# Attention reads and a SoLU feed-forward on one core: w_out split by halves of columns, two tiles turned by TensorE, and a new written-out order

## The chip, the cores and the metric

The kernel runs on one core of a Trainium2 chip. A core has a matrix engine (TensorE, here PE, with PEld for its weight loads), three engines that work on rows of 128 partitions (VectorE or DVE, ScalarE or ACT, GpSimd or POOL), a queue that issues DMA transfers (SyncE, SP), an on-chip memory and eight banks of accumulators that PE writes. Each engine takes its instructions in program order; semaphores tie the engines together. The metric is the device time of one execution in microseconds, lower is better.

## What is computed

```python
def _attn_ref(x, state):                       # x: 8 x 8 x 512 x 64, state: 8 x 8 x 32 x 64
    scores = scale * np.matmul(x, state.transpose(0, 1, 3, 2))
    a = softmax(scores)                        # over the 32 states
    xread = np.matmul(a, state)
    scores2 = scale * np.matmul(state, x.transpose(0, 1, 3, 2))
    a2 = softmax(scores2)                      # over the 512 tokens
    sread = np.matmul(a2, x)
    return np.concatenate([xread, sread], axis=2)

def _moe_ref(x, w_in, w_out, g_ln):            # 4608 rows, 512 -> 1024 -> 512
    h = x @ w_in
    solu = h * softmax(h)
    ln = (solu - mean(solu)) / np.sqrt(var(solu) + 1e-06) * g_ln
    return ln @ w_out
```

The rows of the second function are the reads of the first, heads side by side: 512 token reads and 32 state reads for each of 8 batches. All values are float32, the weights float64.

## The kernel before

The rows are cut into 34 tiles of 128: four tiles of token reads for each batch (tile t belongs to batch t // 4) and two tiles (32, 33) with the state reads of all batches. The token reads are never formed: since xread @ w_in = a @ (state @ w_in), the kernel multiplies the state of each batch with w_in once (V) and takes a from there to h. The work of each tile or batch is a generator, a "step", and the text ORDER names them in the order in which the program is to issue them; `X*n` advances step X n times. No scheduler moves anything after that: what stands earlier in ORDER stands earlier in the queue of its engine. PLACES gives each buffer its slot, and OPT says for each kind of work which engine does which instance (a for ACT, d for DVE, p for POOL). The steps are:

- l, cl, c: a load of half a weight chunk (`raw`, l0 to l7 from w_in, l8 to l15 from w_out), its low words on ACT (L220), and its conversion from float64 on DVE (L231, L234) with an addition on DVE or POOL (L237) into `wf`.
- Ls, LT, Ln, Lg: loads of state, of x in two layouts, and of g (`gT`).
- V{b}{n}: state of batch b times half n of w_in, in two groups of matmuls on PE (L187), each evicted from the accumulators into `swf` (batches 0 and 1) or `vt`. For batches 2 to 7 Y writes that to DRAM, Z reads it back and P splits it into a high and a low part (`swh`, `swl`).
- S{b}: scores on PE (two groups, also L187). A{b}, or Ah{b}{part} for batch 0: the softmax over states on DVE, ACT and POOL, ending in the transposed `aT` (DVE) and, but for batch 0, its parts `ath` and `atl`. E{b}: the softmax over tokens, whose result goes through DRAM; R{b} multiplies it with x (`srps`).
- H{t}: the first product of a tile into an accumulator of two banks (L477), in plain float32 for tiles 0 to 3 and in three products of high and low parts for the others.
- C{t}: from h to the normalised u (maximum on DVE L484, exponential on ACT L487, product on DVE L490, subtraction of the mean L495 or L497, squares on ACT L502, four small steps on POOL L504 to L507).
- D{t}: `bounce`. DVE transposes u in blocks of 32 (`ub`, L514), one DMA writes it to DRAM (`ut`), one reads it back in another layout (`back`).
- T{t}: splits `back` into `uh` and `ul`, in two halves. O{t}: the second product, 24 matmuls of 512 columns into one bank (L545), an eviction with the row scale (`osb`, L552 or L554), and the transfer to the output. Tile 33 does it in two halves of 256 columns.
- wo{f}: the split of chunk f of w_out, scaled by g: `wohi` on ACT (L267), `wolo` on DVE (L271). wp and wi do the same for w_in, which only the last two tiles need.
- K: one small matmul of `ident` with itself (`warm`, L569) whose result nobody reads. It stands where PE would otherwise be idle.

Accumulators: four banks serve h and the V groups of batches 0 and 1, as two buffers of two banks; four serve everything else on PE.

Of the kernel before, what the change touches and what calls it, by code (L numbers as in the profile page):

```python
# [8 lines left out]
F32 = mybir.dt.float32  # L9
# [19 lines left out]
OPT = dict(ph=2, k4=45, direct=[0, 1], hn=[0], vh=[0, 1], ah=[0], add='dpdpdpdpppppppdp', whi='aadd', wlo='dppp',  # L29
           ev='daaaaaaaadaaadaaaaaaaaaaaaaaaaaa', swh='aaaaaaaaadaaaaaa', swl='pppppppppppdddpd', sub='dppddppd',  # L30
           subh='dpdddpdddpdddpdd', mulh='dddddpdddpdddpdd', mul='ppppdpdd', ath='aaaaaddd', alo='dpppppdp',
           up='aaaaaaaaddaaadaaaaaaaaddaadadadadd',
           uh='aaaaaaaadaaaddaaaaaaaaaaadaadaaadaaadaddaaaadaaddaaddadddadaaadadaaa',
           ul='ppddppppdpdppppppddppdppppddpppdpdpppdppppppppdppppdpppdddddppdddddd',
           oe='aaaaaaaaaaaaaadadaaaadadaaaaadaada', hs='aaaaaaaa', jit=[], ed=[0, 1], ec='aaaaaaaaaaaaaaaa')
# [7 lines left out]
c9 c15 c9 c13 E0 cl11 c11 cl8 c8 Lg*2 c13 H0 P10 Ah01 LT20 C0*2 S1 A1*3 Ln00 A1 C0 E1*3 V41 K LT21 cl14 cl9 P11 H1*2
C1 Y31 c9 V41*2 wo4 A1*4 V41 Lg C1*2 V51 K Y21 H3*2 C0*2 D0 C3 V51 C1 D1*2 A1 V51*2 D0 V61 C3 H2*2 C3 R0*2 P10 cl15
Y51 C2 V61 R0 V61 D1 A1 S2 C3 D3 c15 C2*2 wo0 wo2 wo3 wo2 A1 D0 H4*3 c14 H4*3 H5*2 wo1 wo0 wo1 wo3 D3 V61 H5 wo5 H5*3
Z20 c14 T1*2 E1 T1 wo4 O1*2 wo6 O1 wo7 O1*3 wo5 Y50 wo6 C2 T0 T1 C3 D3 O1*3 wo7 T0*2 D2 O0 T0 wp2 O0*2 E2*2 O0 O1 E1
A2 D2 O1*2 E1 O0*5 A2*2 O0*2 C1 T3 Y40 C1 O1 T3*2 LT30 E1*2 C4*2 D2 E2 C0 E2*2 LT31 O0*2 E1 C2 Ln11 T3 E1 O1 A2 E1
Ln10 O3*2 C4*2 O3*2 C5 T2*3 D4*2 C5 E1 C5 A2 O3 R0 O3*5 E2 O0 D4 T2 O3*2 H6*2 A2*2 C2 C3 C5 O2*3 E2 C4 D5*2 wp3 C5 Z21
H6*2 A2 H6*2 wp2 O3*2 P20*2 H7*2 O2*3 C6*3 O2 C6 O2*5 A2 O2 T4 D5 T4 Y41 C5 T4 H7*3 D6*2 H7 C7 O2 S3 R1*3 O4 T4 O4*4
R1 O4*2 wp3 A2 A3*2 P21 C7*2 O4*2 T5 H8*2 Ln21 A2 O4*3 A3 T5 D6 C6 H9*2 C7 D7*2 E2 P21 T5 E2 Z30 H9*2 O5*4 H9*2 D7 E2  # L50
C4 O4 E3 LT40 E3*4 A3*2 LT41 T5 C9*2 T6*2 O5*2 C7 C9*3 D9 O5 H8 O5*2 C7 T6*2 O5 H8*2 A3*2 H8 O5*3 O6*2 O4 O6 P30 O6 D9
O6*2 E3*3 T7 H10*5 T7*3 A3 C8 O6*3 C8*2 O7 C8*2 D8 C6 Z31 P31 O7 Ln20 P31 O6 D9 O6*2 H10 O6 E3 O6 O7*4 A3 C10 O7 D8
# [24 lines left out]
T33*2 O30*3 T30 O30*2 O29 C30 O30 C33 T29 O30 T33 O33*5 T32 O33*3 O29*3 T32 O33*3 T32 O33 C33 O33*9 O32*6 C29*2 O32*4
T32 O32*2 O33 O29*2 C32*2 O32*2 O33*6
# [25 lines left out]
def attention_then_solu_ffn(ctx, tc, xT, xn, stB, w_in, w_out, g, out):  # L104
# [11 lines left out]
    SLOTS = dict(s2=2, m1=1, z1=1, r=1, sc=2, rr=3)  # L116
# [535 lines left out]
```

## Time and profile before

| | |
|---|---|
| device time, median of 3 runs | 352.25 us (350.67 to 353.64) |
| the profiled execution | 350.98 us |
| its span, first to last instruction | 349.2 us |
| busy share: PE, DVE, ACT, POOL | 97%, 79%, 63%, 52% |
| DMA, mean over the span | 270 GB/s |

Busy time is a union over instructions. On PE the end of a matmul is modelled, so prices of matmuls are better taken from start to start. A float32 matmul with float32 operands leaves two records in the profile, one of the split kind (fp32r operands) leaves one. In rows of the timeline equal instructions that follow each other are merged, with their count behind x, and a wait stands in brackets with what ended it.

### The profile page before, as it was taken

What the parts mean: (1) busy time and instruction counts of PE and PEld (TensorE: products, weight loads), DVE (VectorE), ACT (ScalarE), POOL (GpSimd) and SP (SyncE); (2) the same over time, 40 slices, a digit from 0 to 9 for tenths busy, and PEclk for the clock granted to TensorE, in tenths of its full rate; (3) what the DMA queues carried; (4) which work ended last, traced back from release to release, by engine and by line L of the source; (5) the groups of instructions that cost most, each with busy time, mean ns of one, the idle gap of its engine ahead of it and who ended that gap; (6) DMA issues with size and microseconds to landing.
All of it is one profiled execution on the core that took longest, in us unless ns stands there. A gap on an engine that the chain in (4) does not pass through costs nothing.

```text
span 349.2 us, 6119 instructions
## 1 busy us (share of the span) xinstructions
PE 339.0 (97%) x2220; PEld 255.5 (73%) x2220; DVE 274.9 (79%) x386; ACT 220.6 (63%) x356; POOL 182.7 (52%) x241
## 2 busy tenths in 40 slices
PE   5999999999999999999999999999999999999995
PEld 4343335888788867888878778887888888888894
DVE  3889999997888778998779897888787896555720
ACT  3579999889658567578565676555863463544250
POOL 0063594378756764678579463444455518412220
PEclk9899999999999999999999999999999999999999
DMA  7996998899998899999997976897897345344432
GB/s 240 416 402 268 342 322 269 307 294 343 294 363 272 339 363 332 312 329 310 340 327 263 323 247 215 288 306 288 270 297 255 113 150 212 115 167 172 150 107 75
DMA packets 47854, 94.25 MB, mean 270 GB/s; under 512 B 4432, under 2 KB 26192, under 8 KB 47824
## 3 DMA queue, kind: packets, MB, share of 16 engines
q1 hardware_dynamic: 47824, 93.87, 77.8%
q8 instruction: 17, 0.28, 0.3%
q14 instruction: 13, 0.11, 0.1%
HBM read 54.53 MB, written 37.22 MB: 263 GB/s over the span
## 4 chain that ended last, share of the span: by engine, by line
PE 43%; DVE 20%; DMA 15%; ACT 11%; issue 4%; POOL 4%; SPq 1%; DVEq 0%; ACTq 0%; POOLq 0%
PE o L545 28%; PE h L477 13%; DMA back<-ut 7%; DMA out_dram<-osb 3%; DVE u L490 2%; DMA raw<-w_in_dram 2%; DVE sm L484 2%; ACT u L495 2%; DVE wf L234 2%; DVE ub L514 2%; ACT e L487 2%; ACT uh L142 2%; DMA ut<-ub 2%; POOL ul L147 1%; DVE aT L408 1%
## 5 line engine op out<-in xcount | busy, mean ns | idle before, releaser
L147 POOL TENSOR_TENSOR ul<-back,uh 128x512 fp32r<-128x512 f32 x43 | 58.8, 1373 | 66.4 <-ACT uh L142 40.1
L545 PE MATMUL o<-wohi,uh 128*128 128x512 f32 (+1 forms) x280 | 74.8, 385 | 0.6 <-ACT uh L142 0.4
L545 PE MATMUL o<-wolo,uh 128*128 128x512 f32 (+1 forms) x280 | 75.3, 383 | 0.0
L545 PE MATMUL o<-wohi,ul 128*128 128x512 f32 (+1 forms) x280 | 73.6, 383 | 0.0
L545 PEld LDWEIGHTS o<-wohi,uh 128*128 128x128 f32 x280 | 51.5, 188 | 12.1 <-ACT uh L142 1.3
L545 PEld LDWEIGHTS o<-wolo,uh 128*128 128x128 f32 x280 | 51.8, 188 | 10.4
L545 PEld LDWEIGHTS o<-wohi,ul 128*128 128x128 f32 x280 | 51.7, 188 | 10.3
L490 DVE SCALAR_TENSOR_TENSOR u<-h,e 128x1024 f32<-128x1024 f32 x34 | 41.4, 1217 | 22.1 <-ACT e L487 21.2
L487 ACT ACTIVATE e<-h,sm 128x1024 f32<-128x1024 f32 x34 | 37.9, 1113 | 29.0 <-DVE sm L484 28.7
L514 DVE STREAM_TRANSPOSE ub<-u 128x1024 f32<-128x1024 f32 x34 | 42.1, 1237 | 8.3 <-ACT u L495 7.9
L484 DVE TENSOR_REDUCE sm<-h 128x1 f32<-128x1024 f32 x34 | 41.0, 1207 | 8.5 <-PE h L477 4.6
L502 ACT ACTIVATE e<-u 128x1024 f32<-128x1024 f32 x34 | 35.9, 1056 | 9.5 <-DVE u L497 9.2
L142 ACT ACTIVATE uh<-back 128x512 fp32r<-128x512 f32 x48 | 29.0, 623 | 17.2 <-DMA back<-ut 17.2
L495 ACT ACTIVATE u<-u,sm 128x1024 f32<-128x1024 f32 x24 | 27.6, 1149 | 16.4 <-DVE u L490 16.3
L552 ACT ACTIVATE osb<-o,sm 128x512 f32<-128x512 f32 (+1 forms) x29 | 19.2, 663 | 25.4 <-PE o L545 12.1
L477 PE MATMUL h<-swh,ath 128*128 128x512 f32 x112 | 35.1, 395 | 0.0
L477 PE MATMUL h<-swl,ath 128*128 128x512 f32 x112 | 34.5, 389 | 0.0
L477 PE MATMUL h<-swh,atl 128*128 128x512 f32 x112 | 34.5, 389 | 0.0
L237 POOL TENSOR_TENSOR wf<-wf,r 128x512 uint32<-128x512 uint32 x11 | 14.0, 1290 | 27.7 <-DVE wf L234 23.9
L147 POOL TENSOR_TENSOR swl<-swf,swh 128x1024 fp32r<-128x1024 f32 x10 | 24.3, 2432 | 8.0 <-ACT swh L142 5.2
L477 PEld LDWEIGHTS h<-swh,ath 128*128 128x128 f32 x112 | 20.6, 188 | 5.3 <-ACT e L487 0.8
L477 PEld LDWEIGHTS h<-swl,ath 128*128 128x128 f32 x112 | 21.0, 188 | 4.5
(86 smaller groups left out, 496.8 us busy)
## 6 DMA issues: line engine op xcount, KB each, us to landing
ut<-ub SPq DMA_DIRECT2D x34, 512.0 KB, 3.1
back<-ut SPq DMA_DIRECT2D x34, 512.0 KB, 4.9
out_dram<-osb SPq DMA_DIRECT2D x33, 256.0 KB, 4.7
xT<-xT_dram SPq DMA_DIRECT2D x16, 512.0 KB, 8.0
xn<-xn_dram SPq DMA_DIRECT2D x16, 512.0 KB, 7.7
kept<-vt SPq DMA_DIRECT2D x12, 512.0 KB, 6.3
swf<-kept SPq DMA_DIRECT2D x12, 512.0 KB, 6.3
raw<-w_in_dram SPq DMA_DIRECT2D x8, 512.0 KB, 8.4
```

The source lines that it names most:

```text
L142: nc.scalar.activation(out, src, AF.Copy)
L147: engine(k).tensor_tensor(out=out, in0=a, in1=hi.bitcast(F32), op=ALU.subtract)
L237: engine(of("add", n)).tensor_tensor(out=w, in0=w, in1=rounding[n], op=ALU.add)
L477: nc.tensor.matmul(ph[t][:, cols], left[l][:, p, tok], weights[:, cols], start=(p, l, r) == (0, 0, 0), stop=(p, l, r) == (parts - 1, *kind ...
L484: nc.vector.tensor_reduce(nm, ph[t], AX.X, ALU.max, negate=True)
L487: nc.scalar.activation(e, ph[t], AF.Exp, bias=nm, accum_out=z)
L490: nc.vector.scalar_tensor_tensor(out=u, in0=ph[t], scalar=-1.0, in1=e, op0=ALU.mult, op1=ALU.mult, accum_out=su)
L495: nc.scalar.activation(u, u, AF.Identity, bias=su, scale=-float(DF))
L502: nc.scalar.activation(e, u, AF.Square, scale=float(DF) ** -0.5, accum_out=ss)
L514: nc.vector.transpose(ub, us[t][0])
L545: nc.tensor.matmul(po, ut[t][l][:, f, :], w[NP + f // 2][:, f % 2, cols], start=(hf, l, w is wohi, q) == (0, 0, True, 0), stop=(hf, l, q) ...
L552: nc.scalar.activation(o[:, cols], po, AF.Copy, scale=us[t][1])
```

## The change

w_out is loaded and split by halves of its columns, not by chunks of its rows: l8 to l11 now bring the left 256 columns of all eight chunks, l12 to l15 the right 256. wo{m} has three steps: a multiplication by g in place on DVE or POOL, the high part on ACT, the low part on DVE or POOL. Tiles 0 to 3 form their second product in halves, each with its own bank, output buffer and transfer, as tile 33 did. For tiles 0 and 1, D is not `bounce` but `turn_on_pe`: C writes u with its columns permuted (`pu`), PE multiplies its eight chunks with `ident`, and ACT copies the result to `back`. The state is loaded by quarters, not halves. Who does what (OPT), the buffers' slots (PLACES) and the whole order are new.

```diff
-OPT = dict(ph=2, k4=45, direct=[0, 1], hn=[0], vh=[0, 1], ah=[0], add='dpdpdpdpppppppdp', whi='aadd', wlo='dppp',
-           ev='daaaaaaaadaaadaaaaaaaaaaaaaaaaaa', swh='aaaaaaaaadaaaaaa', swl='pppppppppppdddpd', sub='dppddppd',
+OPT = dict(ph=2, k4=45, direct=[0, 1], hn=[0], vh=[0, 1], ah=[0], add='dpppdpddpddddddp', whi='dapd', wlo='ppdd',
+           ev='aaaaaaaaaaaaaaaaaaaaaaaaaaaaaaaa', swh='aaaaaaaappappaad', swl='pppdppdpdpppdppd', sub='ddpppppp',
...
+           oe='aaaaaaaaaaaaaaaaaaaaaaaaaaadaddaaa', jit=[], ed=[0, 1], ec='aaaaaaaaaaaaaaaa', oh=[0, 1, 2, 3, 33],
+           pt=[0, 1], tb='aaaaaaaaaaaaaaaaaaaaaaaaaaaaaaaaaaaaaaaaaaaaaaaaaaaaaaaaaaaaaaaaaaaa', wg='pdddpppd',
+           woh='aaaaaaaa', wol='pddpdddp')
...
-K*5 l0 c0 l2 c2 K*6 c0 c2 cl0 c0 cl2 Ls0 c2 V10 K*3 l6 c6*2 l4 cl6 V20 K V00 K c4*2 cl4 c6 l7 cl7 c4 V00 V20*2 c7*2 l1
+K*2 l2 c2*2 l0 K c0*2 K*5 cl0 cl2 K*2 l6 K c0 K c6*2 Ls0 K l4 K*2 cl6 cl4 K c6 LT00 c2 V00 K*2 c4 K*2 c4 K c4 V10 LT01
...
         else:
-            src = w_out.bitcast(U32).rearrange("(p c f) h -> c f p h", p=4, f=NS)[n - 2 * NP]
-            nc.sync.dma_start(raw[n].rearrange("p h k -> p (h k)"), src)
+            half, i = divmod(n - 2 * NP, NP)
+            src = w_out.bitcast(U32).rearrange("(p c f) h -> c f p h", p=4, f=NS)
+            for c in range(2):
+                nc.sync.dma_start(raw[n].rearrange("p (c h) k -> p c (h k)", c=2)[:, c],
+                                  src[2 * i + c, :, :, half * DM:(half + 1) * DM])
...
+    def split_w_out(m):
+        half, i = divmod(m, NP)
...
+        w = wf[NP + m // 2][:, m % 2].rearrange("p (c h) -> p c h", c=2)
+        engine(of("wg", m)).tensor_tensor(out=w, in0=w, in1=gT[:, 2 * i:2 * i + 2, None].broadcast_to(w.shape), op=ALU.mult)
+        yield
+        hi, lo = (x[NP + i][:, :, half * DM // 2:(half + 1) * DM // 2] for x in (wohi, wolo))
+        copy(of("woh", m), hi, w)
+        yield
+        minus(of("wol", m), lo, w, hi)
+        yield
...
         k = of("up", t)
+        v, into, src = u, u, u
+        if t in OPT["pt"]:
+            v = block([DF], F32, f"pu{t}")
+            into = v.rearrange("x (c f p) -> x p c f", p=4, f=NS)
+            src = u.rearrange("x (p c f) -> x p c f", p=4, f=NS)
         if k == "a":
-            nc.scalar.activation(u, u, AF.Identity, bias=su, scale=-float(DF))
+            nc.scalar.activation(into, src, AF.Identity, bias=su, scale=-float(DF))
...
+    def turn_on_pe(t):
+
+        cols = us[t][0].rearrange("x (c m) -> x c m", c=NFC)
+        for hf in range(2):
+            ps = bank([NFC // 2, P], f"tp{t}_{hf}")
+            for c in range(NFC // 2):
+                nc.tensor.matmul(ps[:, c, :], cols[:, hf * NFC // 2 + c], ident, start=True, stop=True)
+            yield
+            if hf == 0:
+                back[t] = block([NFC, P], F32, f"back{t}")
+            copy(of("tb", 2 * t + hf), back[t][:, hf * NFC // 2:(hf + 1) * NFC // 2], ps)
+            yield
...
-        width = DM // 2 if t == NTILES - 1 else DM
+        width = DM // 2 if t in OPT["oh"] else DM
...
-        step(f"D{t}", bounce, t)
+        step(f"D{t}", turn_on_pe if t in OPT["pt"] else bounce, t)
```

What this moves on the engines, at the two places that matter below. First, PE ahead of the first second product. Before, the last V group and the scores of batch 2 (`sps2`) came there, and then the twelve matmuls each of h4 and h5, of which the first four are shown:

```order
L187 MATMUL swps6_1_1_596<-wf2_151,st2_228 32x512 x2
L187 MATMUL swps6_1_1_596<-wf3_127,st2_228 32x512 x2
L187 MATMUL sps2_0_662<-xT2_0_484,st0_112 32x512 x4
L187 MATMUL sps2_1_663<-xT2_1_522,st0_112 32x512 x4
L477 MATMUL h4_692<-swh1_0_480,ath1_660 128x512 x2
L477 MATMUL h4_692<-swl1_0_643,ath1_660 128x512 x2
L477 MATMUL h4_692<-swh1_0_480,atl1_688 128x512 x2
L477 MATMUL h4_692<-swh1_1_439,ath1_660 128x512 x2
```

Now PE turns tiles 0 and 1 (`tp`) in the middle of h2 and goes on to the second product of tile 1:

```order
L483 MATMUL h2_677<-swf0_0_134,aT0_1_513 128x512 x2
L539 MATMUL tp0_0_693<-ident_74,pu0_609 128x128 x4
L539 MATMUL tp0_1_700<-ident_74,pu0_609 128x128 x4
L539 MATMUL tp1_1_711<-ident_74,pu1_517 128x128 x4
L573 MATMUL o1_0_716<-wohi4_429,uh1_623 128x256 x2
L483 MATMUL h2_677<-swf0_1_135,aT0_1_513 128x512 x2
L573 MATMUL o1_0_716<-wohi5_686,uh1_623 128x256 x2
```

The scores of batch 2, h4 and h5 have moved behind the first halves of the second products of tiles 1 and 0.

Second, DVE from the last exponential of tile 1 on. Before:

```order
L490 SCALAR_TENSOR_TENSOR u1_558,sm1_535<-h1_530,e1_556 128x1024
L514 STREAM_TRANSPOSE ub0_576<-u0_508 128x1024
L484 TENSOR_REDUCE sm3_578<-h3_569 128x1
L514 STREAM_TRANSPOSE ub1_585<-u1_558 128x1024
L408 STREAM_TRANSPOSE aT1_0_589<-a1_0_500 128x1024
L490 SCALAR_TENSOR_TENSOR u3_608,sm3_578<-h3_569,e3_601 128x1024
L484 TENSOR_REDUCE sm2_649<-h2_603 128x1
```

Now, at the place where the softmax of batch 1 (`a1`, `aT1`, `atl1`) ends:

```order
L151 TENSOR_TENSOR ul1_705<-back1_586,uh1_623 128x512
L151 TENSOR_TENSOR wolo5_687<-wf4_317,wohi5_686 128x2x256
L151 TENSOR_TENSOR wolo6_634<-wf5_467,wohi6_633 128x2x256
L411 TENSOR_TENSOR a1_0_276<-a1_0_276,z1_1_0_556 128x1024
L496 SCALAR_TENSOR_TENSOR u3_764,sm3_636<-h3_547,e3_691 128x1024
L414 STREAM_TRANSPOSE aT1_0_782<-a1_0_276 128x1024
L490 TENSOR_REDUCE sm2_788<-h2_677 128x1
L525 STREAM_TRANSPOSE ub3_790<-u3_764 128x1024
L366 TENSOR_REDUCE sc1_264<-se1_265 128x1
L151 TENSOR_TENSOR atl1_816<-aT1_0_782,ath1_786 128x1024
```

The transposes `ub0` and `ub1` are gone, and the end of batch 1's softmax, with its last product now on DVE, has moved behind a part of the split of w_out.

More of the change, by code (lines that the diff above doesn't have):

```diff
@@ L43 @@
[L43 to L52, printed above, removed]
@@ L257, in split_w_in @@
         yield
-    def split_w_out(f):
-        n, q = NP + f // 2, f % 2
-        if q == 0:
-            wohi[n] = block([2, DM], F32R, f"wohi{n}")
-            wolo[n] = block([2, DM], F32R, f"wolo{n}")
-        w, by, hi, lo = wf[n][:, q], gT[:, f:f + 1], wohi[n][:, q], wolo[n][:, q]
-        if of("hs", f) == "a":
-            nc.scalar.activation(hi, w, AF.Copy, scale=by)
-        else:
-            nc.vector.tensor_scalar_mul(hi, w, by)
+    def split_w_out(m):
+        half, i = divmod(m, NP)
+        if half == 0:
+            wohi[NP + i] = block([2, DM], F32R, f"wohi{NP + i}")
+            wolo[NP + i] = block([2, DM], F32R, f"wolo{NP + i}")
+        w = wf[NP + m // 2][:, m % 2].rearrange("p (c h) -> p c h", c=2)
+        engine(of("wg", m)).tensor_tensor(out=w, in0=w, in1=gT[:, 2 * i:2 * i + 2, None].broadcast_to(w.shape), op=ALU.mult)
         yield
-        nc.vector.scalar_tensor_tensor(out=lo, in0=w, scalar=by, in1=hi.bitcast(F32), op0=ALU.mult, op1=ALU.subtract)
+        hi, lo = (x[NP + i][:, :, half * DM // 2:(half + 1) * DM // 2] for x in (wohi, wolo))
+        copy(of("woh", m), hi, w)
+        yield
+        minus(of("wol", m), lo, w, hi)
         yield
@@ L493, in chain @@
         k = of("up", t)
+        v, into, src = u, u, u
[3 more added lines that the diff above has]
+            src = u.rearrange("x (p c f) -> x p c f", p=4, f=NS)
         if k == "a":
-            nc.scalar.activation(u, u, AF.Identity, bias=su, scale=-float(DF))
+            nc.scalar.activation(into, src, AF.Identity, bias=su, scale=-float(DF))
         else:
-            engine(k).tensor_scalar(out=u, in0=u, scalar1=-float(DF), scalar2=su, op0=ALU.mult, op1=ALU.add)
-        us[t] = (u, r)
+            engine(k).tensor_scalar(out=into, in0=src, scalar1=-float(DF), scalar2=su, op0=ALU.mult, op1=ALU.add)
+        us[t] = (v, r)
         yield
-        nc.scalar.activation(e, u, AF.Square, scale=float(DF) ** -0.5, accum_out=ss)
+        nc.scalar.activation(e, v, AF.Square, scale=float(DF) ** -0.5, accum_out=ss)
         yield
@@ L520, in bounce @@
         yield
+    def turn_on_pe(t):
[9 more added lines that the diff above has]
+            yield
     def t_steps(t):
         for hf in range(2):
-            src = back[t].rearrange("p (q c s) -> p c q s", q=4, c=NFC)[:, 4 * hf:4 * hf + 4]
-            part = lambda x: x.rearrange("p c (q s) -> p c q s", q=4)[:, 4 * hf:4 * hf + 4]
+            if t in OPT["pt"]:
+                src = back[t][:, 4 * hf:4 * hf + 4]
+                part = lambda x: x[:, 4 * hf:4 * hf + 4]
+            else:
+                src = back[t].rearrange("p (q c s) -> p c q s", q=4, c=NFC)[:, 4 * hf:4 * hf + 4]
+                part = lambda x: x.rearrange("p c (q s) -> p c q s", q=4)[:, 4 * hf:4 * hf + 4]
             if hf == 0:
@@ L557, in o_steps @@
                 row = (t // NT) * ROWS + (t % NT) * P
-                nc.sync.dma_start(out[row:row + P, cols], o[:, cols])
+                nc.sync.dma_start(out[row:row + P, cols], o)
             else:
@@ L561, in o_steps @@
                 rows = out.rearrange("(b r) d -> r b d", r=ROWS)[S:, b:b + P // NS, cols]
-                nc.sync.dma_start(rows, o[:, cols])
+                nc.sync.dma_start(rows, o)
             yield
@@ L583, in attention_then_solu_ffn @@
         step(f"wo{f}", split_w_out, f)
-    for k in (0, 2):
+    for k in range(B // 2):
         step(f"Ls{k}", load_st, k)
```

112 lines of the change are left out of this document (61 added, 51 removed).

## The prediction

> **What bounds the kernel now.** I read the busy time by stage first, then the waits of TensorE (PE), then its timeline, because PE is the engine with the largest share. Stages, in us from the start of the span (columns: length, then busy time and count of PE, PE's weight loads, DVE, ACT, POOL, then granted clock, DMA share, GB/s):
>
> ```profile
> 8.23:18.37 10.14, 9.34 (x66) 3.16 (x66) 9.07 (x16) 5.26 (x8) 1.62 (x2) 0.83 1.02 412
> 18.37:57.39 39.02, 38.19 (x380) 14.96 (x381) 37.41 (x62) 35.80 (x63) 24.58 (x19) 1.00 0.88 327
> 57.39:345.00 287.61, 287.04 (x1756) 233.21 (x1752) 225.68 (x305) 176.37 (x282) 155.81 (x216) 1.00 0.77 261
> ```
>
> From 57.39 us on PE lacks 0.6 us of being busy all the time; from 18.37 to 57.39 PE, DVE and ACT are all close to full. The list of PE's own waits says the same; these are its longest before and its longest after that point:
>
> ```profile
> PE swph L187 <- DVE wf L237: 2.5, 1, 2.5
> ...
> PE o L545 <- ACT uh L142: 0.4, 1, 0.4
> ```
>
> So after the first loads the end is set by what stands in PE's queue, which runs in program order: a matmul that is added there costs its full price, and a transfer or a DVE instruction that is taken away gives nothing unless PE waited for it. What can still be gained lies ahead of 57 us, in the start and in the filler matmuls (`warm`, step K), which take PE's time like any other. PE's timeline in that part (start, length, line, names, shape, count; a float32 matmul leaves two records, so 10 records of `warm` are five K):
>
> ```profile
> 1.34 4.35 PE L569 MATMUL warm<-ident 128*128 128x128 f32 x22 [1.34 <-POOL ident masks.py:199]
> 8.23 2.52 PE L187 MATMUL swph<-wf,st 64*32 64x512 f32 x8 [2.54 <-DVE wf L237]
> 10.68 1.36 PE L569 MATMUL warm<-ident 128*128 128x128 f32 x6
> ...
> 18.37 1.19 PE L187 MATMUL sps<-xT,st 64*32 64x512 f32 x16 [0.80 <-ACT vt L142]
> ...
> 21.44 1.06 PE L187 MATMUL swps<-wf,st 64*32 64x512 f32 x8
> 22.43 0.94 PE L569 MATMUL warm<-ident 128*128 128x128 f32 x6
> ...
> 25.17 1.38 PE L569 MATMUL warm<-ident 128*128 128x128 f32 x10
> 26.48 1.09 PE L187 MATMUL swps<-wf,st 64*32 64x512 f32 x16
> ...
> 29.22 0.49 PE L569 MATMUL warm<-ident 128*128 128x128 f32 x2
> 29.64 1.09 PE L187 MATMUL swps<-wf,st 64*32 64x512 f32 x16
> 30.66 0.49 PE L569 MATMUL warm<-ident 128*128 128x128 f32 x2
> 30.98 1.88 PE L477 MATMUL h<-swf,aT 128*128 128x512 f32 x4
> 32.80 1.92 PE L187 MATMUL swps<-wf,st 64*32 64x512 f32 x24
> 34.65 0.71 PE L569 MATMUL warm<-ident 128*128 128x128 f32 x4
> ...
> 40.40 3.60 PE L477 MATMUL h<-swf,aT 128*128 128x512 f32 x8
> 43.93 1.09 PE L187 MATMUL swps<-wf,st 64*32 64x512 f32 x16
> ...
> 53.45 1.10 PE L432 MATMUL srps<-xn,e 128*32 128x64 f32 x64
> ...
> 57.39 0.73 PE L477 MATMUL h<-swh,ath 128*128 128x512 f32 x2
> ...
> 62.96 1.07 PE L545 MATMUL o<-wohi,uh 128*128 128x512 f32 x4
> ```
>
> Prices, from start to next start: a run of K costs 0.42 us for one (29.22 to 29.64) and 1.31 for five (25.17 to 26.48), so 0.42 + 0.22 for each further one, 1.09 for four. A V or S group of 8 records costs 0.99 alone (21.44 to 22.43); two in a row 1.02 (29.64 to 30.66), three 1.85 (32.80 to 34.65), and the six from 26.48 to 29.22 2.74, because neighbours overlap. An h tile of batch 0 costs 3.53 (40.40 to 43.93), half of one 1.82 (30.98 to 32.80), R0 1.1. The first second-product matmul (o) starts at 62.96.
>
> The second products at the end of the kernel, where both widths stand side by side:
>
> ```profile
> 329.19 1.07 PE L545 MATMUL o<-wohi,uh 128*128 128x512 f32 x4
> 330.10 1.07 PE L545 MATMUL o<-wolo,uh 128*128 128x512 f32 x4
> ...
> 335.67 0.64 PE L545 MATMUL o<-wolo,uh 128*128 128x256 f32 x4
> ...
> 337.58 0.64 PE L545 MATMUL o<-wohi,ul 128*128 128x256 f32 x4
> ...
> 344.48 0.64 PE L545 MATMUL o<-wohi,ul 128*128 128x256 f32 x4
> ```
>
> A 512-wide matmul costs 0.91 / 4 = 0.227 us, a 256-wide one (337.58 - 335.67) / 16 = 0.119: two halves cost 0.239. The last matmul ends at 344.48 + 0.64 = 345.1; the span ends 4.1 later, at 349.2.
>
> **The change, part by part.**
>
> *Halves.* Tiles 0 to 3 issue 48 narrow matmuls for 24 wide ones: 48 x 0.119 - 24 x 0.227 = 0.27 us each, 1.1 us for four, all of it in PE's full stretch. Their evictions and output transfers are split too; those lie beside PE.
>
> *Turning on PE.* 16 matmuls of 128x128 float32 against `ident`, the form of K: four after half of h3, twelve ahead of the first o. By the K price 1.09 + (0.42 + 11 x 0.2225) = 4.0 us on PE. What it takes away (two DVE transposes of `ub`, four DRAM transfers for tiles 0 and 1) was not what PE waited for: PE spent 57.39 to 62.96 on h4 and h5.
>
> *Fillers.* K stands 41 times instead of 34. Five of the added seven lie ahead of the first V, where PE is idle anyway; behind the first V there are 25 instead of 23, about 0.4 us.
>
> *Loads at the start.* The state comes by quarters and x of batch 0 moves up behind four weight loads. A load of 512 KB lands every 1.33 us in these two waits of ACT, for the fourth and the fifth load:
>
> ```profile
> 9.56 0.68 ACT L220 ACTIVATE r<-raw 128x512 uint32<-128x512 uint32 x1 [2.95 <-DMA raw<-w_in_dram]
> 10.89 0.68 ACT L220 ACTIVATE r<-raw 128x512 uint32<-128x512 uint32 x1 [0.65 <-DMA raw<-w_in_dram]
> ```
>
> S0 now needs 6.5 loads (three weights, half a state load, a weight, two of x): 10.89 + 1.5 x 1.3 = 12.8 us, where S0 started at 18.37. PE's own queue reaches S0 at 12.4 if nothing waits: first V at 8.5 (the same loads and conversions as for 8.23), 0.99, five K 1.31, 0.99, two K 0.64. I take 12.8.
>
> *The clock.* The first V above cost 2.45 us (8.23 to 10.68) for the 0.99 of 21.44, and the clock of that stage was 0.83: PE had stood still for 2.54 us and the clock was cut. With 16 K, at 0.21 to 0.11 us a record, PE now runs to about 6.5 and stands still for 2.0 us. If the clock is cut again, the first V costs 2.45 and the five K some 1.7, and S0 comes at 14.3. The Trainium skill, TensorE: Matmul & The Clock Gate, Part 1, says that the clock falls back after an idle window of about 3.4 us; by that rule neither gap would cut it and S0 stays at 12.8. The trace of before disagrees in its 2.54 us, so the shorter gap stays open. I take the clock as held, three to one.
>
> *From S0 to the first o on PE*, counted in the new order: 22 V and S groups in runs of 2, 1, 3, 2, 1, 1, 1, 6, 3, 2 (13.5 us), 18 K in nine runs (5.8), then h1, h0, both halves of h3 and one of h2 (12.5), four runs of three V groups (7.4), R0 (1.1) and the turns (4.0): 44.2 us. First o at 12.8 + 44.2 = 57.0.
>
> *From there to the end.* Behind its first o, before needed 345.1 - 62.96 = 282.2 us. The new order still has S2 (1.0), h4 and h5 (62.96 - 57.39 = 5.6), the other half of h2 (1.8) and the 1.1 of the halves: 291.7. Last matmul 57.0 + 291.7 = 348.7, which is 3.6 us later than 345.1; with the clock cut 5.1 later. If the one later wait of 0.4 us goes, 3.2. Weighted: +3.8.
>
> *Does DVE deliver in time?* It was full from its first softmax transpose to the first ul; the two rows between show what its kinds cost, 0.63 for a 512-wide transpose (38.00 to 38.63), up to 1.2 where 1024 columns are read:
>
> ```profile
> 19.50 1.44 DVE L388 STREAM_TRANSPOSE a<-sps 128x256 f32<-128x256 f32 x4 [1.11 <-PE sps L187]
> ...
> 38.00 0.70 DVE L408 STREAM_TRANSPOSE aT<-a 128x512 f32<-128x512 f32 x1
> 38.63 1.18 DVE L484 TENSOR_REDUCE sm<-h 128x1 f32<-128x1024 f32 x1
> ...
> 62.50 0.68 DVE L147 TENSOR_TENSOR ul<-back,uh 128x512 fp32r<-128x512 f32 x1
> ```
>
> Priced by kind, that stretch comes to 41.8 us and took 43.0, 3% more. In the new order `atl1`, which h4 needs, is the 81st DVE instruction from the first softmax transpose: about 36 of 512 columns at 0.6, 16 of 1024 at 1.06 to 1.21, 12 conversions at 0.45, eight transposes of 0.36 to 0.63, nine small ones: 51 us, with the 3% 52.4. From 13.8 it comes at 66.2. PE asks for it at 57.0 + 1.8 + 46 x 0.119 + 1.0 + four matmuls of h4 (0.9) = 66.2. No slack: 0 to 1.5 us of wait, which stands in the range. Before, `aT1` stood ahead of the w_out split on DVE; now it stands behind part of it.
>
> *The scattered write of pu.* ACT now writes u of tiles 0 and 1 with neighbours 16 bytes apart. The nearest rows are the same pass with adjacent elements and the one ACT copy that reads scattered elements:
>
> ```profile
> L495 ACT ACTIVATE u<-u,sm 128x1024 f32<-128x1024 f32 x24 | 27.6, 1149 | 16.4 <-DVE u L490 16.3
> ...
> L142 ACT ACTIVATE xrh<-sreadT x1: 2095/2095/2095, 279.9 to 279.9; 128x1024 fp32r<-128x1024 f32 x1
> ```
>
> So 1.15 to 2.1 us each, and I take 2.1, the scattered one: 1.9 us more on ACT for both. The Trainium skill, SBUF — State Buffer, section on the DMA port swizzle, says that SBUF lines are 16 bytes and that each access to a new line pays; by it every element pays, the sum would be the 2.1, and the row of xrh agrees in kind. PE reaches the first turn 12.1 us behind the start of h1 (12.8 + 19.2 + 12.1 = 44.1), while u1, 27 us of DVE instructions behind 13.8, is due at about 41, so this costs PE nothing; it can delay e0 and through it DVE by up to 1 us.
>
> *The rest* (shares between DVE, ACT and POOL, w_out's three-step split, smaller out tiles, casts of uh on POOL) lies beside a full PE; its cover is PE's queue, and if that runs dry it shows as the second rival.
>
> **The rivals.**
> First, the sum stands: +2.6 (no later wait, clock held, S0 at 12.4) to +5.5 us.
> Second, supply fails behind 65 us. The way of a tile through DRAM and back, from the DMA issues (size, median us to landing):
>
> ```profile
> ut<-ub SPq DMA_DIRECT2D x34, 512.0 KB, 3.1
> back<-ut SPq DMA_DIRECT2D x34, 512.0 KB, 4.9
> ```
>
> `ub3` now comes on DVE two places behind `aT1`, at about 65, so its data are back near 74; PE has h4, h5 and o of tiles 0 and 1 until about 76. With 2 us of slack there, and casts on POOL whose duration no row shows, one or two late tiles would add 2 to 5 us: +6 to +10. For it: DVE was 37.4 of 39 us busy; against it: before, with such slacks, only 0.6 us was lost behind 57 us.
> Third, not slower: the 16 turns take one pass, not two, each 0.11 us, 2 us less, and with a held clock and the 0.4 us wait gone the sum is +1.2 us, within 1%. It decides if tp leaves one record for each matmul. Against it: K has the same shape and leaves two (68 records, 34 K). The Trainium skill, TensorE: Matmul & The Clock Gate, Terms, gives float32 a transpose mode four times faster; the code issues a plain matmul, and no run here shows that mode.
> Fourth, faster: the earlier first o (57.0 against 62.96) would count in full, -6 us. It does not, since h4 and h5 only change places with it.
>
> **How the numbers follow.** The profiled execution took 350.98 us around its span of 349.2; the median of the three runs is 352.25, 1.3 more. 352.25 + 3.8 = 356.0. About 1% (3.5 us) is what a measurement of this kernel can tell from no change. Chances: first case 0.62, of which two fifths stay within 3.5 us; second 0.22; third 0.12; faster by over 1% 0.04. So same 0.25 + 0.12 = 0.37, slower 0.37 + 0.22 = 0.59, faster 0.04. Range: from +0.9 (third case, a little below) to +9 (most of the second): 353.1 to 361.5; the first case alone 354.8 to 357.8.
>
> **What would show it.** Right: the first o at 56 to 59 us, sps of batch 0 at 12.4 to 14.3, 32 tp records of 0.11 us, PE busy from there to the end, last matmul 348 to 350. Wrong: PE waiting on uh or ath behind 65 us (second), tp in 16 records (third), or PE's end ahead of 345.

## The result, and the profile after

| | before | after |
|---|---|---|
| device time, median of 4 runs each, taken together | 352.94 us (350.67 to 354.25) | 356.56 us (355.62 to 359.24) |
| after / before, 95% interval | | 1.0115 (1.0072 to 1.0158) |
| the profiled execution | 350.98 us | 355.69 us |
| its span | 349.2 us | 353.9 us |
| last matmul ends | 345.1 us | 350.4 us |

The change makes the kernel 1.15% slower. By the trace PE ends 5.3 us later, and the stretch behind its last matmul is 0.6 us shorter (3.5 for 4.1 us), which leaves 4.7 in the span.

The stages of after, cut at the first V, at the scores of batch 0 and at the first second product (length, then busy time of PE, its weight loads, DVE, ACT, POOL, then granted clock, DMA share, GB/s):

```profile
9.97:15.52 5.55, 5.55 (x31) 3.04 (x31) 2.58 (x5) 1.18 (x2) 0.00 (x0) 0.69 1.03 416
15.52:60.06 44.54, 44.15 (x434) 18.93 (x433) 42.51 (x74) 40.04 (x70) 16.16 (x14) 1.00 0.83 298
60.06:350.40 290.34, 290.34 (x1871) 239.38 (x1869) 222.42 (x291) 168.91 (x273) 192.54 (x252) 1.00 0.73 254
```

From its first second product to its last matmul PE of after is never idle. The list of all of PE's waits is three rows long, and the last of them ends at 26 us:

```profile
PE swph L191 <- DMA st<-stB_dram: 2.1, 1, 2.1
PE warm L596 <- POOL ident masks.py:199: 1.3, 1, 1.3
PE swps L191 <- DVE a L394: 0.4, 1, 0.4
```

So the chain that ended last, in which PE held less than half before, is now almost all PE (share by engine, from the pages of before and of after):

```profile
PE 43%; DVE 20%; DMA 15%; ACT 11%; issue 4%; POOL 4%; SPq 1%; DVEq 0%; ACTq 0%; POOLq 0%
```

```profile
PE 95%; DMA 2%; ACT 1%; SPq 0%; issue 0%; DVE 0%
```

PE's timeline of after, with the rows on which the prediction's times are to be read:

```profile
1.34 6.49 PE L596 MATMUL warm<-ident 128*128 128x128 f32 x32 [1.34 <-POOL ident masks.py:199]
9.97 1.62 PE L191 MATMUL swph<-wf,st 64*32 64x512 f32 x8 [2.14 <-DMA st<-stB_dram]
11.52 2.44 PE L596 MATMUL warm<-ident 128*128 128x128 f32 x10
13.88 1.06 PE L191 MATMUL swph<-wf,st 64*32 64x512 f32 x8
14.88 0.71 PE L596 MATMUL warm<-ident 128*128 128x128 f32 x4
15.52 1.09 PE L191 MATMUL sps<-xT,st 64*32 64x512 f32 x16
...
35.22 3.70 PE L483 MATMUL h<-swf,aT 128*128 128x512 f32 x8
...
48.01 1.05 PE L539 MATMUL tp<-ident,pu 128*128 128x128 f32 x8
48.99 1.92 PE L191 MATMUL swps<-wf,st 64*32 64x512 f32 x24
...
57.46 2.84 PE L539 MATMUL tp<-ident,pu 128*128 128x128 f32 x24
60.06 0.48 PE L573 MATMUL o<-wohi,uh 128*128 128x256 f32 x2
```

The turns take 48.99 - 48.01 = 0.98 and 60.06 - 57.46 = 2.60 us, together 3.58. The first V starts 1.74 us later than before (9.97 for 8.23), and five fillers right behind it take 13.88 - 11.52 = 2.36 us, where five took 1.31 at the full clock. The ledger of the 5.3 us comes from adding up PE's rows by kind, each from its start to the next start:

| | us |
|---|---|
| first V later | +1.7 |
| turns | +3.6 |
| second products (narrow +23.5, wide -22.3) | +1.2 |
| fillers behind the first V, 25 for 23 | +1.4 |
| V groups +0.6, scores -0.8, first products -0.6 | -0.8 |
| waits behind the first V, 0.4 for 2.2 | -1.8 |
| sum | +5.3 |

### The profile page after: what moved, and what is told of

The parts are those of the page before. It is cut to its first block, busy times and chain, and to the rows that moved or that the text cites. A ratio compares the mean times of both kernels' runs of the same rounds, so it can differ in the third digit from the quotient of the medians.

```text
span 353.9 us, 6463 instructions
## 1 busy us (share of the span) xinstructions
PE 346.5 (98%) x2362; PEld 267.7 (76%) x2362; DVE 272.5 (77%) x375; ACT 213.8 (60%) x348; POOL 211.2 (60%) x274
## 4 chain that ended last, share of the span: by engine, by line
PE 95%; DMA 2%; ACT 1%; SPq 0%; issue 0%; DVE 0%
PE o L573 53%; PE h L483 29%; PE swps L191 4%; PE srps L438 2%; DMA st<-stB_dram 2%; PE sps L191 2%; PE warm L596 2%; PE swph L191 2%; PE tp L539 1%; SPq L212 0%; ACT vt L146 0%; DVE a L394 0%; ACT se L372 0%; ACT r L227 0%; ACT a L403 0%
## 5 line engine op out<-in xcount | busy, mean ns | idle before, releaser
L151 POOL TENSOR_TENSOR ul<-back,uh 128x512 fp32r<-128x512 f32 x49 | 67.5, 1381 | 46.5 <-ACT uh L146 25.4
L573 PE MATMUL o<-wohi,ul 128*128 128x512 f32 (+1 forms) x312 | 76.1, 362 | 0.0
L573 PEld LDWEIGHTS o<-wohi,uh 128*128 128x128 f32 x312 | 54.8, 189 | 9.8 <-issue 0.5
L573 PEld LDWEIGHTS o<-wohi,ul 128*128 128x128 f32 x312 | 54.9, 189 | 9.5
L573 PEld LDWEIGHTS o<-wolo,uh 128*128 128x128 f32 x312 | 54.3, 189 | 9.0
L496 DVE SCALAR_TENSOR_TENSOR u<-h,e 128x1024 f32<-128x1024 f32 x34 | 41.4, 1217 | 16.8 <-ACT e L493 13.9
L525 DVE STREAM_TRANSPOSE ub<-u 128x1024 f32<-128x1024 f32 x32 | 39.6, 1238 | 7.4 <-ACT u L506 6.5
L579 ACT ACTIVATE osb<-o,sm 128x512 f32<-128x512 f32 (+1 forms) x36 | 22.4, 623 | 31.9 <-PE o L573 20.7
L146 ACT ACTIVATE uh<-back 128x512 fp32r<-128x512 f32 x32 | 19.9, 629 | 26.0 <-DMA back<-ut 24.1
L506 ACT ACTIVATE u<-u,sm 128x1024 f32<-128x1024 f32 x20 | 23.0, 1150 | 17.4 <-DVE u L496 16.7
L483 PEld LDWEIGHTS h<-swh,atl 128*128 128x128 f32 x112 | 20.8, 188 | 4.3
```

Source lines behind the costliest of these rows:

```text
L146: nc.scalar.activation(out, src, AF.Copy)
L151: engine(k).tensor_tensor(out=out, in0=a, in1=hi.bitcast(F32), op=ALU.subtract)
L483: nc.tensor.matmul(ph[t][:, cols], left[l][:, p, tok], weights[:, cols], start=(p, l, r) == (0, 0, 0), stop=(p, l, r) == (parts - 1, *kind ...
L496: nc.vector.scalar_tensor_tensor(out=u, in0=ph[t], scalar=-1.0, in1=e, op0=ALU.mult, op1=ALU.mult, accum_out=su)
L506: nc.scalar.activation(into, src, AF.Identity, bias=su, scale=-float(DF))
L525: nc.vector.transpose(ub, us[t][0])
```

## The experiments

The theory is that of the prediction: PE's in-order queue sets the end, so what stands in it costs its full price. The rivals are that the added matmuls lie in time in which PE would wait, that the supply of tiles decides, and that the start does. "First o" is the first second product, "h1" the first product of tile 1, S0 and S1 are the scores of batches 0 and 1, and times of matmuls are those of the one execution of each kernel that was profiled. Ratios are to the kernel before in the same set of runs. That kernel's medians were 352.83, 353.25 and 352.83 us in the three sets, four, four and two experiments long.

### The turns twice

```diff
-                nc.tensor.matmul(ps[:, c, :], cols[:, hf * NFC // 2 + c], ident, start=True, stop=True)
+                for _ in range(2):
+                    nc.tensor.matmul(ps[:, c, :], cols[:, hf * NFC // 2 + c], ident, start=True, stop=True)
```

> The kernel after with each of the 16 turning matmuls issued twice. Theory, PE's queue sets the end: the 16 added ones take what the first 16 took, 3.6 us (0.98 + 2.60 in the profile of after), and the last matmul moves from 350.4 to 354.0, +1.0%; 64 records of tp. Rival, the turns lie in time that PE would spend waiting for the tiles' data anyway: less than 1 us more.

359.19 us, ratio 1.0184 (1.0157 to 1.0211), 0.7% above after's, where 1.0% was expected. The trace has 64 tp records:

```profile
47.53 1.95 PE L540 MATMUL tp<-ident,pu 128*128 128x128 f32 x16
49.40 1.92 PE L191 MATMUL swps<-wf,st 64*32 64x512 f32 x24
...
57.87 5.52 PE L540 MATMUL tp<-ident,pu 128*128 128x128 f32 x48
63.15 0.48 PE L574 MATMUL o<-wohi,uh 128*128 128x256 f32 x2
```

They take 49.40 - 47.53 = 1.87 and 63.15 - 57.87 = 5.28 us, together 7.15, 3.57 more than in after. From S0, here at 15.04, to the first o it is 48.11 us for 44.54, again 3.57 more: the doubled turns come out at their full price. The last matmul ends at 354.00, 3.60 later, but that this is the same number is chance: S0 came 0.5 earlier than in after, and 0.5 were lost again behind the first o, in small steps between 225 and 255 us.

### All second products in halves

```diff
-                        nc.tensor.matmul(po, ut[t][l][:, f, :], w[NP + f // 2][:, f % 2, cols],
...
+                        for p0 in range(0, width, DM // 2):
+                            part = slice(p0, p0 + DM // 2)
+                            from_w = slice(at + p0, at + p0 + DM // 2)
+                            nc.tensor.matmul(po[:, part], ut[t][l][:, f, :], w[NP + f // 2][:, f % 2, from_w],
...
```

> The kernel after with the second product of all 34 tiles in matmuls of 256 columns: tiles 4 to 32 too, both halves into one bank, with one eviction and one transfer as in after. 29 tiles x (48 x 0.119 - 24 x 0.227) = 7.8 us more on PE. Theory, PE's queue sets the end and a narrow matmul costs 0.119: +7.8 us, +2.2%. Rival, behind 65 us the supply of tiles has slack to lose or the narrow ones cost half a wide one: within 0.5%.

364.02 us, ratio 1.0333 (1.0307 to 1.0359), 2.2% above after's. On PE the second products take 196.3 us instead of 187.9, 8.4 more: 0.29 us for each of the 29 tiles, where 0.27 was worked out. The last matmul ends at 358.7, 8.3 later, but the first o was 1.3 earlier (58.76), since the clock was not cut at the start of this run: behind the first o PE took 9.6 us more. The 1.2 beyond the second products lie in the first products that stand between them (103.3 us for 102.1); why these became longer stays open. The narrow matmul's price and the theory hold; halves everywhere cost PE more than the sum by that price.

### No fillers behind the first V, in both kernels

In after (in before likewise):

```diff
-LT00 c2 V00 K*2 c4 K*2 c4 K c4 V10 LT01 K*2 S0
+LT00 c2 V00 c4*3 V10 LT01 S0
...
```

> The kernel after without the 25 filler matmuls K that stand behind its first V (the 16 ahead of it stay). In the profile of after the fillers behind the first V took 8.85 us of PE from start to start. Theory, PE's queue is full and every instruction in it counts: the fillers count too, but those ahead of h1 stand where PE would otherwise wait for scores and their softmax, so a part comes back as waits; the last matmul 3 to 7 us earlier than 350.4, time -1 to -2%. Rival, fillers only fill: PE waits behind the first V grow by as much as the fillers took, h1 starts at 35.2 as in after, and the time is the same within 0.5%.

> The kernel before without the 23 filler matmuls K behind its first V, which took 7.43 us of PE there. Theory: as for after, 2 to 6 us off the last matmul at 345.1, the rest comes back as waits on the softmax of batch 0. Rival, fillers only fill: no change, h0 starts at 31.0 as in before.

After without fillers: 354.5 us, 1.0054 (1.0028 to 1.0081); first o at 57.38, last matmul at 348.52, 1.9 us earlier for 8.85 us of fillers, less than the 3 to 7 expected. Its ratio is 0.6% below after's, with intervals that overlap. Before without fillers: 354.42 us, 1.0043 (1.0006 to 1.0079), not faster; in the profiled executions its last matmul even moved from 345.1 to 348.6. PE's waits in before without fillers show what came in their place:

```profile
PE swph L186 <- DVE wf L236: 4.1, 2, 2.2
PE sps L186 <- ACT vt L141: 2.1, 1, 2.1
PE o L544 <- ACT uh L141: 1.8, 1, 1.8
...
PE sps L186 <- DVE sr L435: 1.2, 1, 1.2
PE swps L186 <- ACT se L141: 1.2, 1, 1.2
```

Of the first row 1.9 us lie ahead of the first V, and the wait of the third row lies at 242 us, far behind the fillers. In before the rival is right: h0 starts at 30.6 for 31.0, and the 7.43 us of fillers came back ahead of the first o as 6.2 us more of waits and 1.6 us in V groups, some of them at the half clock. In after 2.7 us reach the first o. The rest came back behind the first V, 3.1 us as waits, almost all of it in the one wait below, and 3.2 in V and score groups, at the half clock: the emptier queue was cut twice, where after was cut once (below).

```profile
PE sps L190 <- DMA xT<-xT_dram: 3.2, 1, 3.2
```

Of the 2.7 us 0.8 were lost again behind the first o.

### More fillers ahead of the first V

```diff
-LT00 c2 V00
+LT00 c2 K*8 V00
```

> The kernel after with 24 instead of 16 filler matmuls ahead of its first V; nothing else changed. In the five profiles so far the clock was decided in steps of 3.41 us from the moment it first rose: it was halved for a step after each step in which PE was busy 1.43 us or less (0.91, 1.27, 1.10, 1.29, 1.43, 0.46) and not after 1.51 or more. Theory, S0 was late by the cut clock: with the gap ahead of the first V cut from 2.1 to 0.3 to 1.6 us no step is that empty, the clock stays full, the first V costs 0.99 and not 1.55, the five K behind it 1.3 and not 2.4, S0 starts at about 13.9 instead of 15.52, and the last matmul comes up to 1.6 us earlier than 350.4. Rival, the stretch behind S0 is set by loads and by DVE: S0 earlier, but h1 at 35.2 and the end as in after, within 0.5 us.

354.84 us, 1.0058 (1.0020 to 1.0095), 0.6% below after's ratio. The start of PE, as its timeline shows it:

```profile
9.81 1.06 PE L190 MATMUL swph<-wf,st 64*32 64x512 f32 x8
10.80 1.38 PE L595 MATMUL warm<-ident 128*128 128x128 f32 x10
...
13.75 1.09 PE L190 MATMUL sps<-xT,st 64*32 64x512 f32 x16
...
21.70 1.20 PE L190 MATMUL sps<-xT,st 64*32 64x512 f32 x16 [0.75 <-DMA xT<-xT_dram]
```

S0 stands at 13.75 (13.9 expected), and the clock was not cut. First o and last matmul are each 1.3 us earlier than in after; of the 1.77 gained at S0 0.5 was lost again, to the wait for x of batch 1. Eight added fillers thus brought the end of PE forward: they kept the clock up in a stretch in which PE had nothing to do.

One cut lowers the mean granted clock of an execution by 0.005 (3.41 us at half of 354), so each execution tells whether it was cut. All ten with 24 fillers have 0.998 to 1.000. Of the twelve of after, of the turns twice and of all tiles in halves, which have the same start with 16 fillers, seven have 0.993 to 0.995 (all four of after among them) and five 1.000 (the kernel with tile 1 bounced, which has this start too, is cut again later and is not counted). So the eight fillers prevent a cut that otherwise comes in some executions and not in others. That the whole kernel is faster by it is likely and not shown: the intervals of the two ratios overlap, and the cut and the uncut executions of the turns twice do not differ clearly (359.28 and 359.09 us against 359.33 and 358.12).

### The state quarter loaded third

```diff
-l6 K c0 K c6*2 Ls0
+Ls0 l6 K c0 K c6*2
```

> The kernel after with the first quarter of the state loaded third, ahead of the third piece of w_in. In after the first V waited for it until 9.84, while the weights it needs were ready at 9.04 (the addition on POOL, 7.24 and 1.80 long). Theory: the first V at 9.1, 0.9 earlier; S0 not before its own loads at 13.6, so 13.7 to 15; the last matmul 0.5 to 1.5 us earlier than 350.4. Rival: the piece of w_in that is now later holds the second V group and DVE's conversions, and nothing is gained (within 0.5 us).

354.77 us, 1.0033 (0.9999 to 1.0066). The first V came at 8.08 (9.1 expected), its second half only at 9.20, behind an addition to `wf` on POOL that ended at 9.15. S0 came at 13.13 (its second half waited for x), first o at 58.77, where the run with 24 fillers had 58.76, and the last matmul at 349.79, 0.6 earlier than in after. The clock was not cut in any of the ten executions (0.998 to 1.000), so what the earlier V is worth beside the uncut clock stays open. What the two runs share is the bound behind it: S0 needs loads that landed at 13.5 us, and the scores of batch 1 start at 21.7 in both. Behind the first o this run lost 0.7 us that the run with 24 fillers did not lose.

### Tile 1 by DVE and DRAM again

```diff
-           pt=[0, 1]
+           pt=[0]
...
-P10 C1 Lg
+P10 C1 D1*2 C1 Lg
...
-c15 c13 Y30
+c15 c13 D1 Y30
```

> The kernel after with tile 1 turned by DVE and a way through DRAM again, tile 0 by PE as in after; the DVE transposition stands right behind the last pass over u1. Theory, PE's queue sets the end and the turn of a tile costs it 1.8 us: eight matmuls less, 16 records of tp; the way over DRAM (u1 at 45.7, turned 46.9, then 3 + 5 us and the split, against the first o at 60.06) fits ahead of the first o, and the last matmul comes 1 to 1.8 us earlier than 350.4. Rival, supply: PE waits for uh1 or ul1 by as much as it saves or more, since SP sends seven other transfers in between; same or slower than after.

362.05 us, 1.0272 (1.0213 to 1.0330): the rival, and more than it said. ACT, SP's queue and PE in that kernel:

```profile
60.90 0.63 ACT L145 ACTIVATE uh<-back 128x512 fp32r<-128x512 f32 x1 [4.92 <-DMA back<-ut]
```

```profile
45.23 0.33 SPq L336 DMA_DIRECT2D ut<-ub  x1
...
47.55 6.14 SPq L313 DMA_DIRECT2D kept<-vt  x5
53.78 0.42 SPq L341 DMA_DIRECT2D back<-ut  x1
```

```profile
62.07 3.79 PE L538 MATMUL tp<-ident,pu 128*128 128x128 f32 x16 [4.67 <-ACT vt L145]
```

The way over DRAM took from 45.2 to 60.9 us, not 8: its second transfer stood in SP's queue behind five writes of V and went out at 53.78. ACT's queue stopped at uh1 for 4.9 us; evictions of V and the high parts of w_out stood behind it, and PE waited 4.7 us ahead of the turn of tile 0 for a bank that ACT was to empty. The wait also cut the clock, for 6.8 us from 60.21 on: the 16 tp records took 65.50 - 62.07 = 3.43 us instead of 1.8. The first o came at 65.50, 5.4 later than in after, although S0, with an uncut clock, stood 1.8 earlier. At this place of this order the turn on PE costs 1.8 us a tile and saves more than that. That does not make it a gain over before, whose PE did other work in that time.

### Fewer fillers, other work in their place

Three attempts at a faster kernel. The first takes all fillers behind the first V away, puts 21 ahead of it, loads the state third and puts the addition of the piece l2 of w_in on DVE, with the first two steps of V30 ahead of S1:

```diff
-K*2 l2 c2*2 l0 K c0*2 K*5 cl0 cl2 K*2 l6 K c0 K c6*2 Ls0 K l4 K*2 cl6 cl4 K c6 LT00 c2 V00
+K*8 l2 c2*2 l0 Ls0 c0*2 cl2 c2 cl0 c0 l6 K*13 c6*2 l4 cl6 cl4 c6 LT00 V00
...
-LT10 E0 S1 E1 E0 E1 l7 c1 K Ah00 E0 A1*2 V30 l8 K V30*2 c7*2 K cl7 V30
+LT10 E0 V30*2 S1 E1 E0 E1 l7 c1 Ah00 E0 A1*2 l8 V30 c7*2 cl7 V30
...
```

The second is the kernel with 24, without the six fillers behind S1:

```diff
-S1 E1 E0 E1 l7 c1 K Ah00 E0 A1*2 V30 l8 K V30*2 c7*2 K cl7
+S1 E1 E0 E1 l7 c1 Ah00 E0 A1*2 V30 l8 V30*2 c7*2 cl7
...
```

The third is the kernel with 24 fillers, with only seven more, and with work drawn ahead of S1. (In the first and the third the moved groups have other banks in PLACES.)

```diff
-V20*4 V10 c5 K*3 Ah00 LT11 Ah01 K LT10 E0 S1 E1 E0 E1 l7 c1 K Ah00 E0 A1*2 V30 l8 K V30*2 c7*2 K cl7 V30 V21 K c7 cl8 V21*2 c8 Ah01*2 Ah00 V01
+V20*4 V10 c5 Ah00 l7 LT11 Ah01 LT10 E0*2 c1 Ah00 V30*4 c7*2 cl7 c7 E0 l8 V21*4 S1 E1*2 A1*2 cl8 c8 Ah01*2 Ah00 V01
...
```

> The kernel after without fillers behind its first V, with 21 ahead of it, the state quarter loaded third, the addition of the second piece of w_in on DVE and ahead of the third piece's conversion, and the first half of V of batch 3 ahead of the scores of batch 1, where the kernel without fillers waited 3.2 us for x. Theory, what counts is PE's full queue from about 22 us on plus its waits ahead of that: the first V at 8.4 to 9.1, the clock full throughout, the wait of 3.2 down to 1.2, and the last matmul 4 to 6 us earlier than the 348.5 of the kernel without fillers, 343 to 345, time 1 to 1.5% below before. Rival, DVE's conversions and softmax set the stretch up to h1: h1 at 31 to 32.5 as there, and the last matmul at 347 to 348.5.

> The kernel with 24 fillers ahead of the first V (last matmul at 349.1 in its profile), without the six fillers that stand behind the scores of batch 1, where PE waited for nothing; they took 6 x 0.42 = 2.5 us there. Theory, from there PE's queue is full and each instruction in it counts, as long as the clock stays full: last matmul at 346.6 to 347.2, 2 to 2.5 us earlier, ratio to the kernel before 0.997 to 1.001. Rival, the fillers covered waits for DVE and ACT (the conversions of the last pieces of w_in, the softmax of batch 0), as those of the kernel before did: h1 at 33.9 as with them, or a wait of 1 us or more ahead of h1, and the time as with them.

> The kernel with 24 fillers ahead of the first V, with only the seven ahead of the scores of batch 0 behind it; in place of the others real work is drawn forward: the last piece of w_in is loaded and converted ahead of the scores of batch 1, and both V groups of batch 3 and the right half of batch 2 go ahead of these scores too, evicted at once. Theory, PE has work whenever it waited so far: h1 at 29.5 to 31.5 instead of 33.9, last matmul at 345 to 347, ratio to the kernel before 0.992 to 1.000. Rival, DVE sets h1 (its softmax of batch 0 ended at 29.9 in the kernel without fillers and is now behind a conversion) and PE's waits cut the clock: h1 at 32 or later, last matmul at 347.5 or later.

| | time, us | ratio (interval) | first o | last matmul |
|---|---|---|---|---|
| first | 355.18 | 1.0074 (1.0046 to 1.0102) | 60.20 | 350.55 |
| second | 354.78 | 1.0066 (1.0034 to 1.0098) | 57.78 | 349.83 |
| third | 358.9 | 1.0164 (1.0125 to 1.0204) | 60.85 | 354.99 |

All three missed what was expected of them. In the first, PE waited 2.5 us for x ahead of S1 and 1.6 us behind it, and the clock was cut for 10.2 us. In the second, the six fillers (2.5 us) brought the first o forward by 1.0: 1.2 came back as waits for DVE (transposed scores 0.6, a conversion 0.6). Then 1.7 us were lost behind the first o, though nothing had been changed there, in part here:

```profile
159.55 1.20 PE L572 MATMUL o<-wohi,uh 128*128 128x512 f32 x4 [0.29 <-ACT uh L145]
171.16 1.20 PE L572 MATMUL o<-wohi,uh 128*128 128x512 f32 x4 [0.43 <-ACT uh L145]
```

Between 157 and 183 us PE fell 1.3 us behind the kernel with 24 fillers, and the run with the state first lost 0.5 us in the same place. So the supply of tiles has next to no slack there. In the third, PE waited 3.9 us, at 20 to 24 us, for one conversion whose addition is on POOL, and 3.8 more were lost behind the first o, 1.5 of them in one wait for `uh` at 255.7 us. No version that beats the kernel before was found.

## Why the prediction was right

The forecast was 356.0 us (353.1 to 361.5), slower by over 1% the likeliest; measured were 356.56 us and +1.15%. Its first case took place: the mechanism was right, PE's queue is full and what was added to it sets the end. That the sum came out within 0.6 us is luck in part: the start failed by 2.7 us, and gains that were not foreseen made up for most of it. Of the signs that were set for the first case, 32 tp records of 0.11 us and a busy PE came; S0 (15.52 for 12.4 to 14.3), first o (60.06 for 56 to 59) and last matmul (350.40 for 348 to 350) lay outside.

- *In-order PE.* Right, and shown: twice the turns cost 3.6 us more, all tiles in halves 8.4 us more on PE, and behind the first o PE of after never waited.
- *Halves.* 1.1 us forecast, 1.2 in the ledger.
- *Turns.* 4.0 forecast, 3.58 found. They leave 32 records, so the rival of a single pass falls.
- *Fillers.* The step "about 0.4 us" counted them. In the ledger they were 1.4, because the five behind the first V ran at the half clock. And "takes PE's time like any other" holds only where PE has nothing to wait for: of after's 8.85 us, 2.7 reached the first o when they were taken out; of before's 7.43, nothing.
- *First V at 8.5.* Failed: 9.97. The term "the same loads and conversions as for 8.23" left out that the state quarter now came fourth; the first V waited for it until 9.84. The conversions were not the same either: OPT moved the addition of l2 from DVE to POOL, where it took 1.80 us and ended at 9.04.

```profile
7.24 1.80 POOL L244 TENSOR_TENSOR wf<-wf,r 128x512 uint32<-128x512 uint32 x1 [5.95 <-ACT r L227]
```

- *The clock held, three to one.* Failed: it was cut. The shorter gap of 2.1 us was enough. S0 came at 15.52, later than both values given (12.8 and 14.3). Against the 12.4 us of PE's own queue, 1.5 come from the first V and 1.6 from matmuls at half the clock, 5.55 from the first V to S0 for 3.94 with 24 fillers. The loads of S0 took longer as well: x was there at 13.64 and not at 12.8, since the state quarter, counted as half a load, landed 2.2 us behind the load ahead of it. Of the 2.7 us 1.8 could be had: with 24 fillers S0 stands at 13.75, held by PE's queue behind a first V at 9.81, and 0.3 behind its loads. Three to one was too sure: of the twelve executions above that have this start seven were cut.
- *From S0 to the first o.* 44.2 forecast, 60.06 - 15.52 = 44.5 found.
- *From there to the last matmul.* 291.7 forecast, 290.3 found. Of the difference 0.6 are the two waits (0.4 and 0.2) that before had there and after has not; the rest stays open. The tail behind it, 0.6 us shorter, was not in the sum. The sum was +3.6 with the clock held; the 2.7 us of the start, the 0.3 behind it and these 2.0 that went the other way give the +4.7 of the profiled executions, up to rounding. Between the medians it is +3.6, where +3.8 was forecast.
- *DVE and atl1.* Both engines were to meet at 66.2. The DVE row below ends at 68.9, and PE used it at 69.27, 0.4 us later; both had moved with S0, and no wait arose.

```profile
L151 DVE TENSOR_TENSOR atl<-aT,ath x1: 1211/1211/1211, 67.7 to 67.7; 128x1024 fp32r<-128x1024 f32 x1
```

- *The scattered write of pu.* 2.1 forecast; the row (min/median/max in ns) shows 2.26 for 1.15. The Trainium skill, SBUF — State Buffer, section on the DMA port swizzle, has each access that crosses to a new 16-byte line pay a penalty. The row agrees with that in kind.

```profile
L506 ACT ACTIVATE pu<-u,sm x2: 2237/2260/2284, 44.5 to 52.2; 128x1024 f32<-128x1024 f32 x2
```

- *Supply as a rival.* It did not decide in after. But it was near: the bounced tile cost 4.7 us of waiting at once, and of the kernels whose first o came earlier, three lost 0.7 to 1.7 us again behind it (state third, no fillers, six fillers less). The run with 24 fillers lost none.
- *Faster by the earlier first o.* The first o came 2.9 us earlier than before, and the end 5.3 later, since h4, h5 and the scores of batch 2 only moved behind it.

## What to carry to other kernels

Where one engine's queue is full to the end, price an edit by what it puts into that queue. Ahead of that stretch, first ask what the engine waits for, since there fillers and their removal are nearly free. A filler is worth its time where an otherwise idle stretch would cut the clock, and worth little as a reserve to be cashed in: taken out, most of it came back as waits and as matmuls at the half clock. A hop over DRAM is not its two transfers but these plus the queue in front of the second.

## What the runs showed of the hardware

The cut of TensorE's clock goes by fixed steps of 3.41 us, not by the length of a gap. The steps are counted from when the clock first rises, which was between 4.18 and 7.48 us in these profiles. Each pair below is a step and the one behind it (length, PE busy, other engines, granted clock). After:

```profile
6.94:10.35 3.41, 1.27 (x12) 0.88 (x15) 3.09 (x5) 0.88 (x2) 1.80 (x1) 1.00 0.84 287
10.35:13.76 3.41, 3.41 (x18) 2.21 (x10) 2.34 (x4) 0.67 (x1) 0.00 (x0) 0.50 1.02 416
```

The turns twice, and all tiles in halves:

```profile
6.23:9.65 3.42, 1.44 (x15) 1.27 (x18) 3.20 (x5) 1.81 (x3) 1.77 (x1) 1.00 0.94 291
9.65:13.06 3.41, 3.41 (x16) 1.82 (x9) 3.01 (x5) 0.68 (x1) 0.00 (x0) 0.50 1.02 416
```

```profile
5.36:8.77 3.41, 1.72 (x15) 1.53 (x14) 3.17 (x5) 1.92 (x3) 1.39 (x1) 1.00 0.90 247
8.77:12.18 3.41, 2.41 (x22) 1.48 (x26) 3.10 (x5) 0.68 (x1) 0.39 (x1) 1.00 1.03 419
```

All tiles in halves waited longer ahead of its first V than after (2.7 for 2.1 us) and was not cut, because its gap fell across two steps. Over the twelve profiles the clock was halved behind every step with PE busy for 0.46 to 1.44 us, and behind none with 1.51 to 2.4, but for one with 1.62, far later in before without fillers, which the rule in the expectation for 24 fillers had left out. So whether the same start is cut hangs on how the steps fall on it, as the clocks of single executions above show. Once cut, it also stays cut behind a half-busy step, as in the first of the three attempts:

```profile
17.13:20.54 3.41, 1.31 (x15) 0.18 (x8) 3.39 (x8) 3.41 (x8) 0.47 (x2) 1.00 1.02 405
20.54:23.95 3.41, 2.07 (x16) 0.37 (x16) 1.67 (x3) 1.50 (x5) 2.67 (x3) 0.50 1.06 350
23.95:27.37 3.42, 1.95 (x12) 0.24 (x12) 2.90 (x5) 2.93 (x7) 0.00 (x0) 0.50 0.89 238
27.37:30.78 3.41, 3.25 (x32) 0.91 (x40) 3.38 (x9) 1.79 (x3) 1.30 (x1) 0.50 1.04 395
```

The Trainium skill, TensorE: Matmul & The Clock Gate, Part 1, speaks of a free-running window of 3413 ns, and the steps agree with that. The prediction had read its idle window as a gap of that length; by these rows a step that is 42% busy counts as idle.
